# An attention and feed-forward kernel: new cuts at the end and in w_out, pair 0's loads on one queue, the first software load behind GpSimd's constants, five stores in halves

## Chip, cores and metric

One core of a Trainium2 chip. The metric is the device time of one execution in microseconds (us). A kernel is timed several times; medians are given with the lowest and highest run. The profile comes from one execution of each kernel, and its "span" runs from the first to the last instruction that the trace holds. The measured time is about 2 us longer than the span, that difference called **outside the span** below. The granted clock is the share of its full clock that the chip grants TensorE.

## The reference

Linear attention in 8 batches, 8 heads, 576 rows and 64 columns, an RMS norm, then a feed-forward part on 4608 tokens:

```python
kv  = einsum('bhsd,bhse->bhde', k, v)
out = einsum('bhsd,bhde->bhse', q, kv)
x   = out / sqrt(mean(out*out, -1) + 1e-6) * g_norm     # then (4608, 512)
h   = x @ w_in                                          # 512 -> 2048
out = (h / (1 + exp(-1.702*h))) @ w_out                 # 2048 -> 512
```

## The kernel before

Heads are treated in pairs: four pairs per batch, "pair 0" being the first. TensorE runs the feed-forward part tile by tile (9 tiles of 512 tokens), with the attention of later batches fitted in between. What the change touches:

```python
LAST = ((0, DM // 2), (DM // 2, DM))          # last projection: 256 + 256 columns
...
for n in "kqv":                               # pair 0 of batch 0, f32, two hardware queues
    dst, src = ...
    if n == "v":
        nc.sync.dma_start(out=dst[:, 0:1], in_=src[:, 0:1])
        nc.scalar.dma_start(out=dst[:, 1:2], in_=src[:, 1:2])
    else:
        (nc.sync if n == "k" else nc.scalar).dma_start(out=dst, in_=src)
g_row = const.tile([1, D], F32)
nc.scalar.dma_start(out=g_row, in_=g_norm.unsqueeze(0))
nc.vector.memset(ident, 0.0)
nc.vector.memset(kvb[1], 0.0)
early_load("q", 0, 1, 2)                      # first load of GpSimd's software queue
nc.gpsimd.affine_select(out=ident, ...)       # the mask
...
for c in range(1, NPAIR):                     # pairs 1 to 3, software queue, f32 -> f16
    for n in "qkv"[c == 1 :]:
        early_load(n, 0, c, c + 1)
load_w_in(...)                                # five requests, same queue
nc.vector.memset(ones2, 0.0)                  # and two blocks of ones
...
def project(mo, fo): ...                      # one matmul of 512 columns into os[mo]
def store_rest(mo, n0, n1):                   # one store on Sync, one on ScalarE
    ...
    queue = (nc.sync, nc.scalar)[g]
    queue.dma_start(out=rows, in_=osb[g * R : (g + 1) * R, mo, n0:n1])
def project_last(mo):
    for i, (n0, n1) in enumerate(LAST):       # 16 matmuls, copy, store
        ...
        copy = nc.vector.tensor_copy if i else nc.scalar.copy
        copy(osb[:, mo, n0:n1], o)
        store_rest(mo, n0, n1)
if deep:                                      # tile 0
    steps = [(mo, 4 * i + k) for i in range(4) for mo in range(4) for k in range(4)]
...
elif t < B:                                   # tiles 2 to 7: one store of 1 MB
    nc.sync.dma_start(out=out[t * S : t * S + SM, :].rearrange(...), in_=osb)
...
for c in (0, 2):
    load_half("k", 1, c, c + 2)
    load_half("v", 1, c, c + 2)
    load_w_out(8 + 2 * c, 12 + 2 * c)         # last quarter of w_out in one request
```

Of the kernel before, what the change touches and what calls it, by code (L numbers as in the profile page):

```python
# [8 lines left out]
F32 = mybir.dt.float32  # L9
# [3 lines left out]
P = 128  # L13
# [3 lines left out]
def kernel(  # L17
# [10 lines left out]
    nc = tc.nc  # L28

    B, H, S, D = q.shape  # L30
    DM = H * D
    DFF = moe_w_in.shape[1]
    NPAIR = H // 2
    FO = DFF // P
    KO = DM // P
    EPS = 1e-6
    SM = 512
    J = SM // P
    R = S - SM
    assert R == 64 and B * R == SM and KO == NPAIR and 2 * D == P  # L40
    NT = B + 1
    LAST = ((0, DM // 2), (DM // 2, DM))
    EARLY = 2
    PE_ = 96
    NJ = S // PE_
# [11 lines left out]
    opool = ctx.enter_context(tc.tile_pool(name="opool", bufs=2))  # L57
# [18 lines left out]
    ones2 = const.tile([P, P], F16)  # L76
# [10 lines left out]
    def early_src(n, b, c0, c1):  # L87
        return srcs[n][b, 2 * c0 : 2 * c1].rearrange("h (p j) d -> p h (j d)", j=NJ)

    def early_load(n, b, c0, c1):  # L90
        nc.gpsimd.dma_start(  # L91
            out=raw[n][0:PE_, c0:c1, :].rearrange("p c (l x) -> p (c l) x", l=2),
            in_=early_src(n, b, c0, c1),
        )
# [15 lines left out]
    def load_half(n, b, c0, c1):  # L110
        for l in range(2):
            nc.gpsimd.dma_start(  # L112
                out=raw[n][l * PH : (l + 1) * PH, c0:c1, 0 : NH * D],
                in_=srcs[n][b].rearrange("(c l) (p j) d -> l p c (j d)", l=2, j=NH)[l][:, c0:c1],
            )
# [5 lines left out]
    def load_q(b, queue=nc.sync):  # L121
        t = stage.tile([P, H, J * D], F32, name="qf", tag="qf")
        queue.dma_start(out=t, in_=q[b, :, 0:SM, :].rearrange("h (p j) d -> p h (j d)", j=J))
        r = stage.tile([P, 4, D], F32, name="qrf", tag="qrf")
        for g in range(2):
            queue.dma_start(
                out=r[g * R : (g + 1) * R],
                in_=q[b, 4 * g : 4 * g + 4, SM:S, :].rearrange("h p d -> p h d"),
            )
        staged[b] = (t, r)  # L130
# [12 lines left out]
    for n in "kqv":  # L143
        first[n] = stage.tile([P, H, J * D], F32, name=f"{n}f", tag=f"{n}f")
        first[n] = first[n].rearrange("p h x -> p (h x)")[0:PE_, 0 : 2 * NJ * D]
        dst, src = first[n].rearrange("p (h x) -> p h x", h=2), early_src(n, 0, 0, 1)
        if n == "v":
            nc.sync.dma_start(out=dst[:, 0:1], in_=src[:, 0:1])
            nc.scalar.dma_start(out=dst[:, 1:2], in_=src[:, 1:2])
        else:  # L150
            (nc.sync if n == "k" else nc.scalar).dma_start(out=dst, in_=src)
    g_row = const.tile([1, D], F32)
    nc.scalar.dma_start(out=g_row, in_=g_norm.unsqueeze(0))
    nc.vector.memset(ident, 0.0)
    nc.vector.memset(kvb[1], 0.0)
    early_load("q", 0, 1, 2)
    nc.gpsimd.affine_select(
        out=ident,
        in_=ident,
# [3 lines left out]
        pattern=[[-1, P]],  # L163
        channel_multiplier=1,
    )
    def load_w_in(f0, f1, k0=0, k1=KO):
        nc.gpsimd.dma_start(
            out=w_in_sb[:, k0:k1, f0 * P : f1 * P],
            in_=moe_w_in[k0 * P : k1 * P, f0 * P : f1 * P].rearrange(
                "(ko ki) f -> ki ko f", ki=P  # L170
            ),
        )

    for c in range(1, NPAIR):
        for n in "qkv"[c == 1 :]:
            early_load(n, 0, c, c + 1)
    load_w_in(0, 4, 0, 2)
    load_w_in(0, 4, 2, KO)
    load_w_in(4, GROUP)
# [1 line left out]
    load_w_in(10, FO)  # L181

    nc.scalar.preload_act_table_set("natural_log_exp_and_others")
    nc.vector.memset(ones2, 0.0)
    nc.vector.memset(ones2[0:D, 0:D], 1.0)
    nc.vector.memset(ones2[D:P, D:P], 1.0)
    nc.vector.memset(eps_t, EPS)
    one_t = const.tile([1, 1], F32)
    nc.vector.memset(one_t, 1.0)
# [2 lines left out]
    def load_w_out(f0, f1):  # L192
        nc.gpsimd.dma_start(
            out=w_out_sb[:, f0:f1, :],
            in_=moe_w_out[f0 * P : f1 * P, :].rearrange("(fo ki) n -> ki fo n", ki=P),
        )
# [252 lines left out]
    def dense(t, units1, units2, group, deep, hid=None):  # L449
        hid = hid or Hidden(t)  # L450
        gT = hid.gT
        if group and t:
            order = [(ko, fo) for part in (range(4), range(4, group)) for ko in (0, 1) for fo in part]
            order += [(ko, fo) for ko in range(2, KO) for fo in range(group)]
            for ko, fo in order:
                pool = (ps_h, "hT") if fo < 3 else (ps_a, "att") if fo == 3 else (ps_o, "o")
                hid.mm(ko, fo, *pool)
            for fo in range(group):
                hid.gate(fo)
        for fo in range(FO):  # L460
            if fo >= group:
                for ko in range(KO):
                    hid.mm(ko, fo)
                hid.gate(fo)
            for u in units1.get(fo, ()):
                u()

        osb = opool.tile([P, 4, DM], F32, name="osb", tag="osb")
        os = {}

        def project(mo, fo):
            if fo == 0:
                pool, tag = (ps_h, "hT") if deep and mo < 2 else (ps_o, "o")
                os[mo] = pool.tile([P, DM], F32, name="o", tag=tag)
            nc.tensor.matmul(  # L475
                os[mo],
                gT[:, fo, mo * P : (mo + 1) * P],
                w_out_sb[:, fo, :],
                start=(fo == 0),
                stop=(fo == FO - 1),  # L480
            )
            if fo == FO - 1:
                by_act = mo % 2 if deep or t == B else 0 < t < B - 1 and mo < 2
                copy = nc.scalar.copy if by_act else nc.vector.tensor_copy
                copy(osb[:, mo, :], os[mo])  # L485
                if t == B:
                    store_rest(mo, 0, DM)

        def store_rest(mo, n0, n1):
            for g in range(2):  # L490
                rows = out[(2 * mo + g) * S : (2 * mo + g + 1) * S, n0:n1]
                if 2 * mo + g < EARLY:
                    p0 = SM % PE_
                    rows = rows[bass.DynSlice(NJ * p0 + SM // PE_, R, step=NJ), :]
                else:
                    rows = rows[SM:S, :]
# [5 lines that stand above are left out]
            for i, (n0, n1) in enumerate(LAST):  # L502
                o = ps_a.tile([P, n1 - n0], F32, name="oh", tag="att")
                for fo in range(FO):
                    nc.tensor.matmul(  # L505
                        o,
                        gT[:, fo, mo * P : (mo + 1) * P],
                        w_out_sb[:, fo, n0:n1],
                        start=(fo == 0),
                        stop=(fo == FO - 1),  # L510
                    )
                copy = nc.vector.tensor_copy if i else nc.scalar.copy
                copy(osb[:, mo, n0:n1], o)
                store_rest(mo, n0, n1)

        if deep:
            steps = [(mo, 4 * i + k) for i in range(4) for mo in range(4) for k in range(4)]
        else:
            steps = [(mo, fo) for mo in range(4 - (t == B)) for fo in range(FO)]
        for n, (mo, fo) in enumerate(steps):  # L520
            project(mo, fo)
            for u in units2.get(n, ()):
                u()
        if t == B:
            project_last(3)
        if t < EARLY:

            n = 0
            while n < SM:
                mo, j, p = n // P, n // PE_, n % PE_  # L530
                m = min((mo + 1) * P, (j + 1) * PE_) - n
                nc.sync.dma_start(
                    out=out[t * S : (t + 1) * S, :][bass.DynSlice(NJ * p + j, m, step=NJ), :],
                    in_=osb[n % P : n % P + m, mo, :],
                )
                n += m
        elif t < B:
            nc.sync.dma_start(
                out=out[t * S : t * S + SM, :].rearrange("(p j) m -> p j m", j=J), in_=osb
            )  # L540


    a0 = First(0)
# [70 lines left out]
    for c in (0, 2):  # L614
        load_half("k", 1, c, c + 2)
        load_half("v", 1, c, c + 2)
        load_w_out(8 + 2 * c, 12 + 2 * c)
    load_q(2, nc.gpsimd)

    nc.gpsimd.dma_start(out=g_all, in_=g_norm.unsqueeze(0).to_broadcast([P, D]))  # L620

    live = {0: a0}

    def start(b):
# [2 lines left out]
    for t in range(NT):  # L627
# [32 lines left out]
        elif b < B:  # L660
# [21 lines left out]
            at2(36, of(b, "ss", NPAIR))  # L682
            at2(36, of(b, "apply", NPAIR))
        dense(t, u1, u2, (GROUP, 5)[t] if t < 2 else 0, t == 0, None if t else d0)


# [28 lines left out]
```

## Time and profile before

| | before |
|---|---|
| time, median of 3 runs | 287.84 us (287.82 to 288.01) |
| span of the profiled run | 285.6 us |
| that run's time outside the span | 2.14 us |
| TensorE's last matmul ends | 281.65 us |
| end of the span after that, the "tail" | 3.94 us |

The tail and the time outside are worked out from the trace's nanoseconds: 285.595 - 281.654, and 287.74 (the profiled run) - 285.595. The views round, so a tail here and below can differ by 0.01 from what they give.

In the lines of the profile PE is TensorE, PEld its weight loads, DVE VectorE, ACT ScalarE, POOL GpSimd and SP Sync; L91 is line 91 of the kernel, x4 a count. The DMA issues of the first 2.4 us (destination and source, queue, count, KB each, us from issue to landing). ACTq is ScalarE's queue, SPq is Sync's, POOLq is GpSimd's software queue:

```profile
kf<-in_k_dram SPq DMA_DIRECT2D x1, 288.0 KB, 4.4
qf<-in_q_dram ACTq DMA_DIRECT2D x1, 288.0 KB, 4.6
vf<-in_v_dram SPq DMA_DIRECT2D x1, 144.0 KB, 4.8
vf<-in_v_dram ACTq DMA_DIRECT2D x1, 144.0 KB, 5.1
qraw<-in_q_dram POOLq DMA_DIRECT2D x1, 144.0 KB, 5.5
```

All five requests are open together. The timelines (start, us, engine, line, operation, in brackets the idle time before it and what ended it) show when GpSimd makes the first software request, and how TensorE meets the last of w_out:

```profile
1.29 0.82 POOL L91 DMA_DIRECT2D qraw<-in_q_dram  x1 [0.84 <-POOLq L699]
...
42.13 1.29 PE L475 MATMUL o<-w_out_sb,gT 128*128 128x512 f16 x4
43.26 0.38 PE L259 MATMUL outT<-qT,kvb 128*128 128x512 f16 x1
```

### The profile page before, as it was taken

What the parts mean: (1) busy time and instruction counts of PE and PEld (TensorE: products, weight loads), DVE (VectorE), ACT (ScalarE), POOL (GpSimd) and SP (SyncE); (2) the same over time, 40 slices, a digit from 0 to 9 for tenths busy, and PEclk for the clock granted to TensorE, in tenths of its full rate; (3) what the DMA queues carried; (4) which work ended last, traced back from release to release, by engine and by line L of the source; (5) the groups of instructions that cost most, each with busy time, mean ns of one, the idle gap of its engine ahead of it and who ended that gap; (6) DMA issues with size and microseconds to landing.
All of it is one profiled execution on the core that took longest, in us unless ns stands there. A gap on an engine that the chain in (4) does not pass through costs nothing.

```text
span 285.6 us, 4343 instructions
## 1 busy us (share of the span) xinstructions
PE 278.9 (98%) x1717; PEld 135.4 (47%) x1717; DVE 119.3 (42%) x233; ACT 156.1 (55%) x273; POOL 56.0 (20%) x78
## 2 busy tenths in 40 slices
PE   7899999999999999999999999999999999999994
PEld 2444544455445544554455445544454444444443
DVE  2540656527651757156713862286327400110011
ACT  2697349766565646574558436762666375026400
POOL 8931541111211121112011401140002000000000
PEclk9999999999999999999999999999999999999999
DMA  8999999995589339963698269924501220021022
GB/s 175 204 205 205 206 251 238 234 268 103 123 166 254 58 73 197 252 116 73 191 197 176 37 186 171 228 54 147 119 2 37 73 112 0 0 92 57 0 73 73
DMA packets 53349, 38.76 MB, mean 136 GB/s; under 512 B 31138, under 2 KB 50850, under 8 KB 52562
## 3 DMA queue, kind: packets, MB, share of 16 engines
q0 software_dynamic: 14944, 15.58, 32.7%
q1 hardware_dynamic: 37664, 21.94, 31.0%
q10 hardware_dynamic: 722, 0.97, 1.2%
q8 instruction: 13, 0.21, 0.3%
q14 instruction: 6, 0.05, 0.0%
HBM read 36.73 MB, written 9.44 MB: 162 GB/s over the span
## 4 chain that ended last, share of the span: by engine, by line
PE 85%; DMA 11%; ACT 1%; POOL 1%; DVE 0%; issue 0%
PE o L475 39%; PE hT L438 39%; DMA w_out_sb<-in_moe_w_out_dram 10%; PE kvp L227 2%; PE outR L291 2%; DMA qf<-in_q_dram 2%; PE oh L505 1%; PE ss L339 1%; PE idle L554 0%; PE q L393 0%; POOL vbuf L112 0%; PE outT L259 0%; ACT qraw L545 0%; PE outT L270 0%; POOL qraw L91 0%
## 5 line engine op out<-in xcount | busy, mean ns | idle before, releaser
L475 PE MATMUL o<-w_out_sb,gT 128*128 128x512 f16 x560 | 130.9, 379 | 0.1
L447 ACT ACTIVATE gT<-hT 128x512 f16<-128x512 f32 x144 | 84.5, 599 | 76.5 <-PE hT L438 76.4
L438 PE MATMUL hT<-xT,w_in_sb 128*128 128x512 f16 x512 | 116.2, 379 | 0.0
L438 PEld LDWEIGHTS <-w_in_sb 128*128 128x128 f16 x576 | 54.5, 98 | 62.3 <-DMA w_in_sb<-in_moe_w_in_dram 0.5
L475 PEld LDWEIGHTS <-gT 128*128 128x128 f16 x560 | 52.8, 98 | 56.5 <-issue 0.7
L485 DVE COPY osb<-o 128x512 f32<-128x512 f32 x20 | 13.8, 691 | 62.3 <-PE o L475 62.3
L323 POOL TENSOR_TENSOR x<-xr,g_all 128x512 f16<-128x512 f32 x12 | 15.3, 1272 | 71.2 <-DVE xr L316 47.2
L218 DVE COPY kpad<-kraw 64x576 f16<-64x576 f16 x56 | 25.0, 446 | 2.0 <-DMA kraw<-in_k_dram 0.7
L302 DVE TENSOR_REDUCE sum<-sq 128x8 f32<-128x512 f16 x24 | 15.8, 679 | 19.9 <-ACT sq L299 19.9
L240 DVE CAST kvb<-kvp 64x128 f16<-64x128 f32 x28 | 8.1, 288 | 36.5 <-PE kvp L227 36.3
L316 DVE TENSOR_TENSOR xr<-outR,sum 128x512 f32<-128x512 f32 x24 | 15.5, 686 | 11.1 <-ACT sum L313 11.1
L112 POOL DMA_DIRECT2D kraw<-in_k_dram x16 | 9.9, 624 | 49.4 <-DVE kpad L218 43.5
L112 POOL DMA_DIRECT2D vbuf<-in_v_dram x16 | 9.7, 608 | 34.0 <-PE kvp L227 29.3
L323 DVE TENSOR_TENSOR x<-xr,g_all 128x512 f16<-128x512 f32 x12 | 15.2, 1268 | 0.7
L299 ACT ACTIVATE sq<-outR 128x512 f16<-128x512 f32 x24 | 13.6, 590 | 2.0 <-PE outR L291 1.6
L227 PEld LDWEIGHTS <-kpad 128*128 128x128 f16 x252 | 11.0, 98 | 7.0 <-DVE kpad L218 0.9
L438 PE MATMUL hT<-x_rem,w_in_sb 128*128 128x512 f16 x64 | 14.0, 379 | 0.0
L279 ACT ACTIVATE sq<-outT 128x512 f16<-128x512 f32 (+1 forms) x16 | 7.7, 481 | 10.5 <-PE outT L259 9.1
L485 ACT COPY osb<-o 128x512 f32<-128x512 f32 x15 | 8.7, 581 | 6.3 <-DMA out_dram<-osb 6.3
L227 PE MATMUL kvp<-vbuf,kpad 128*128 128x64 f16 x252 | 11.9, 193 | 0.1
L312 ACT ACTIVATE sum<-sum,eps_t 128x16 f32<-128x16 f32 x12 | 3.7, 308 | 15.0 <-DVE sum L302 15.0
L341 ACT ACTIVATE ln<-ss,eps_t 128x512 f32<-128x512 f32 (+1 forms) x16 | 9.4, 584 | 4.2 <-PE ss L339 4.1
(62 smaller groups left out, 140.8 us busy)
## 6 DMA issues: line engine op xcount, KB each, us to landing
out_dram<-osb SPq DMA_DIRECT2D x6, 1024.0 KB, 4.3
qf<-in_q_dram SPq DMA_DIRECT2D x5, 1024.0 KB, 8.4
kraw<-in_k_dram POOLq DMA_DIRECT2D x12, 288.0 KB, 5.9
vbuf<-in_v_dram POOLq DMA_DIRECT2D x12, 288.0 KB, 6.1
w_out_sb<-in_moe_w_out_dram POOLq DMA_DIRECT2D x4, 512.0 KB, 14.1
out_dram<-osb SPq DMA_DIRECT2D x6, 192.0 KB, 5.6
qf<-in_q_dram POOLq DMA_DIRECT2D x1, 1024.0 KB, 12.7
kraw<-in_k_dram POOLq DMA_DIRECT2D x7, 144.0 KB, 9.5
```

Source lines behind the costliest of these rows:

```text
L112: nc.gpsimd.dma_start(out=raw[n][l * PH : (l + 1) * PH, c0:c1, 0 : NH * D], in_=srcs[n][b].rearrange("(c l) (p j) d -> l p c (j d)", l=2, ...
L218: nc.vector.tensor_copy(out=kpad[r, c, :, l * D : (l + 1) * D], in_=kraw[r, c, 0 : NH * D].rearrange("p (j d) -> p j d", j=NH),)
L227: nc.tensor.matmul(self.kvp[:, c, :], kpad[:, c, j, :], vbuf[:, c, j * D : (j + 1) * D], start=(j == 0), stop=(j == NH - 1),)
L299: nc.scalar.activation(sq, t, AFT.Square)
L302: nc.vector.tensor_reduce(out=self.sum2[:, j % 2, :], in_=sq.rearrange("p (h d) -> p h d", h=H), op=ALU.add, axis=mybir.AxisListType.X,)
L316: nc.vector.tensor_mul(xr[:, i], self.o[j + i].rearrange("p (h d) -> p h d", h=H), s2[:, i, :].unsqueeze(2).to_broadcast([P, H, D]),)
L323: (nc.vector if i else nc.gpsimd).tensor_mul(self.x16[:, j + i, :].rearrange("p (h d) -> p h d", h=H), xr[:, i], g_all.unsqueeze(1).to_bro ...
L341: nc.scalar.activation(ln[:, 0:n], t[:, 0:n], AFT.Ln, bias=eps_t, scale=1.0 / D)
L438: nc.tensor.matmul(self.h[fo], w_in_sb[:, ko, fo * P : (fo + 1) * P], self.x[:, ko], start=(ko == 0), stop=(ko == KO - 1),)
L447: nc.scalar.activation(self.gT[:, fo, :], self.h[fo], AFT.Gelu_apprx_sigmoid)
L475: nc.tensor.matmul(os[mo], gT[:, fo, mo * P : (mo + 1) * P], w_out_sb[:, fo, :], start=(fo == 0), stop=(fo == FO - 1),)
L485: copy(osb[:, mo, :], os[mo])
```

## The change

Its intent: copy and store less after the last matmul; take the last wait for w_out away; let pair 0's loads run through one hardware queue in the order of use; and keep the software queue's first load out of their way until GpSimd has written its constants. In addition the stores of tiles 2 to 6 go out in halves. The diffs here and below are shortened: `...` and words in brackets stand for what is left out. `store(t, j0, j1)` is one request on Sync for the rows j0 to j1 of a tile.

```diff
-    LAST = ((0, DM // 2), (DM // 2, DM))
+    LAST = ((0, 3 * P), (3 * P, DM))
@@ pair 0
-        if n == "v":
-            nc.sync.dma_start(out=dst[:, 0:1], in_=src[:, 0:1])
-            nc.scalar.dma_start(out=dst[:, 1:2], in_=src[:, 1:2])
-        else:
-            (nc.sync if n == "k" else nc.scalar).dma_start(out=dst, in_=src)
+        nc.sync.dma_start(out=dst, in_=src)
@@ GpSimd
-    early_load("q", 0, 1, 2)
     nc.gpsimd.affine_select(...)
+    nc.gpsimd.memset(ones2, 0.0)
+    nc.gpsimd.memset(ones2[0:D, 0:D], 1.0)
+    nc.gpsimd.memset(ones2[D:P, D:P], 1.0)
-        for n in "qkv"[c == 1 :]:
+        for n in "qkv":
-    nc.vector.memset(ones2, 0.0)                  (and its two blocks)
@@ stores
+                elif t in HALVED and mo % 2:      # HALVED = (2, 3, 4, 5, 6)
+                    store(t, mo - 1, mo + 1)
-        elif t < B:
-            nc.sync.dma_start(out=out[...], in_=osb)
+        elif t < B and t not in HALVED:
+            store(t, 0, J)
@@ tile 0's projection
-            steps = [(mo, 4 * i + k) for i in range(4) for mo in range(4) for k in range(4)]
+            steps = [(mo, 4 * i + k) for i in range(3) for mo in range(4) for k in range(4)]
+            steps += [(mo, f + k) for f in (12, 14) for mo in range(2) for k in range(2)]
+            steps += [(mo, 12 + k) for mo in (2, 3) for k in range(4)]
@@ w_out
-        load_w_out(8 + 2 * c, 12 + 2 * c)
+        if c == 0:
+            load_w_out(8, 12)
+        else:
+            load_w_out(12, 14)
+            load_w_out(14, FO)
```

More of the change, by code (lines that the diff above doesn't have):

```diff
@@ L183 @@
     nc.scalar.preload_act_table_set("natural_log_exp_and_others")
-    nc.vector.memset(ones2, 0.0)
-    nc.vector.memset(ones2[0:D, 0:D], 1.0)
-    nc.vector.memset(ones2[D:P, D:P], 1.0)
     nc.vector.memset(eps_t, EPS)
@@ L466, in dense @@
                 u()
-        osb = opool.tile([P, 4, DM], F32, name="osb", tag="osb")
+        osb = osbs[t] = opool.tile([P, 4, DM], F32, name="osb", tag="osb")
         os = {}
@@ L536, in dense, with store @@
                 n += m
-        elif t < B:
-            nc.sync.dma_start(
-                out=out[t * S : t * S + SM, :].rearrange("(p j) m -> p j m", j=J), in_=osb
-            )
+        elif t < B and t not in HALVED:
+            store(t, 0, J)
+    def store(t, j0, j1):
+        nc.sync.dma_start(
+            out=out[t * S : t * S + SM, :].rearrange("(p j) m -> p j m", j=J)[:, j0:j1],
+            in_=osbs[t][:, j0:j1],
+        )
     a0 = First(0)
@@ L616 @@
         load_half("v", 1, c, c + 2)
-        load_w_out(8 + 2 * c, 12 + 2 * c)
+        if c == 0:
[3 more added lines that the diff above has]
+            load_w_out(14, FO)
     load_q(2, nc.gpsimd)
     nc.gpsimd.dma_start(out=g_all, in_=g_norm.unsqueeze(0).to_broadcast([P, D]))
+    osbs = {}
+    HALVED = (2, 3, 4, 5, 6)
     live = {0: a0}
```

## The prediction

> **What bounds the kernel now.** I read the page first (engine shares and the chain that ended last), then the tables by stretch, the timeline of TensorE and of GpSimd, and the waits of TensorE and its weight loads.
>
> ```profile
> span 285.6 us, 4343 instructions
> PE 278.9 (98%) x1717; PEld 135.4 (47%) x1717; DVE 119.3 (42%) x233; ACT 156.1 (55%) x273; POOL 56.0 (20%) x78
> PE 85%; DMA 11%; ACT 1%; POOL 1%; DVE 0%; issue 0%
> ```
>
> TensorE is busy 98% of the span, with two large groups of 576 and 560 matmuls of 512 columns at a pace of 0.216 us (64 of them take 13.81 us in the chain). The change adds and removes no such matmul. So all that can move is the rest: the start, the few stalls of TensorE on loads, and the tail after its last matmul. The run is 287.84 us for a span of 285.6, so I carry 2.2 us outside the span as a constant.
>
> The start, from the table by stretch (columns: PE, PEld, DVE, ACT, POOL busy, granted clock, DMA share, GB/s moved):
>
> ```profile
> 2.00:3.00 1.00, 1.00 (x4) 0.35 (x3) 0.00 (x0) 0.73 (x1) 0.91 (x3) 1.00 0.67 166
> 3.00:3.50 0.50, 0.50 (x3) 0.22 (x2) 0.00 (x0) 0.50 (x1) 0.50 (x2) 1.00 1.03 390
> 3.50:4.00 0.50, 0.50 (x3) 0.18 (x2) 0.00 (x0) 0.06 (x1) 0.50 (x2) 1.00 1.13 313
> 4.00:4.50 0.50, 0.50 (x3) 0.15 (x1) 0.00 (x0) 0.00 (x0) 0.50 (x2) 1.00 1.11 252
> 5.50:6.00 0.50, 0.42 (x2) 0.00 (x0) 0.17 (x1) 0.50 (x1) 0.50 (x2) 1.00 1.28 203
> 7.00:12.00 5.00, 4.81 (x86) 2.56 (x85) 2.72 (x8) 2.94 (x6) 4.86 (x8) 1.00 1.31 200
> ```
>
> From 3.0 us the DMA engines are full (share over 1). The 200 GB/s from 5.5 us on is not slower: those loads read f32 and write f16, and the count is of the bytes written, so some 400 GB/s are read. TensorE looks busy here, but 21 of its matmuls are dummies that keep it warm. What really holds it is the stream of loads:
>
> ```profile
> 12.82 0.38 PE L376 MATMUL kv<-vbuf,kraw 96*64 96x64 f16 x12 [0.67 <-DMA vbuf<-in_v_dram]
> 16.36 4.90 PEld L438 LDWEIGHTS <-w_in_sb 128*128 128x128 f16 x24 [0.28 <-DMA w_in_sb<-in_moe_w_in_dram]
> 23.34 4.94 PEld L438 LDWEIGHTS <-w_in_sb 128*128 128x128 f16 x24 [0.24 <-DMA w_in_sb<-in_moe_w_in_dram]
> ```
>
> Pair 3's v ends a wait of 0.67 us at 12.8, then w_in chunks end waits of 0.28 and 0.24. Whatever TensorE wins before 12.8 us beyond that 0.67 is lost again, unless the stream itself comes earlier. The last such meeting is the chain of waits around 42 us:
>
> ```profile
> 33.04 9.53 DMA w_out_sb<-in_moe_w_out_dram
> 42.57 0.04 issue
> 42.61 0.81 PE o L475 x3
> ```
>
> The last quarter of w_out is requested at 33.04 and lands at 42.57. The TensorE timeline has 4 matmuls from 42.13 where the next piece starts at 43.26: 1.13 us for 4 x 0.216 = 0.86, so a stall of 0.27. After that TensorE shows no wait at all until its end at 281.65. The tail:
>
> ```profile
> 281.65 0.02 issue
> 281.68 0.42 DVE osb L513
> ```
>
> then the store of the second half (issue at 282.1) and the end at 285.6.
>
> **What the Trainium skill says.** "DMA: Bandwidth & Descriptors", section "Issuing engines are not separate DMA queues": loads started on several engines run on the same 16 DMA engines and interleave; more queues save sequencer time only. The trace agrees: with two hardware queues and the software queue the engines are simply full from 3.0 us. So putting k, q and v on one queue changes their order, not the sum of the work. Same page, "Queues, rings and completion order": each engine takes the queues in turn by packet; that the fourth load then shares with pair 0 fits the first software load's 5.5 us to landing, against 5.0 for the next. "TensorE: Matmul & The Clock Gate", section "Back-to-back issue gap", gives some 81 ns a matmul at 128 columns in a real stream; this trace has 9 products of 64 columns with new weights in 0.26 us (29 ns each) and 12 transposes of 96 columns in 0.40 (33 ns), so the measurement decides and I take 55 ns at 128 columns. "VectorE: DVE Perf Modes", section "Zero memsets can be issued as uint32", explains the row of 128x64 uint32 in 0.112 us for a 128x128 f16 zero; on GpSimd the same memset is f16 and no run here shows its length yet.
>
> **The change, part by part.**
>
> 1. End: the last projection is cut 384 + 128 columns, not 256 + 256. TensorE: 16 x (0.163 + 0.055) = 3.49 us against 32 matmuls in 3.51 in the chain: nothing. The last VectorE copy shrinks from 256 to 128 columns. A 512-column copy takes 0.69 and a 256-column one 0.42, so 0.27 for 256 columns, and 0.42 - 0.13 = 0.29: **-0.13 us**. The last two stores carry 32 KB, not 64; stores of 64 KB land in 2.1 us and of 128 KB in 2.4 to 2.7, so perhaps **-0.05**, since at this size most is fixed. The larger first part: TensorE ends it 16 x 0.055 = 0.88 us before the last matmul, the ScalarE copy of 384 columns is between 0.37 and 0.58 (0.48), and each store issue takes some 0.5, so the queues are free 0.1 after TensorE's end, before the last copy ends at 0.31. No new wait.
>
> 2. w_out in two requests of 256 KB, and the projection of tile 0 ordered so that its last quarter is first used as chunks 12 and 13 for two row blocks, then 14 and 15. At 200 GB/s written, 256 KB take 1.3 us: chunks 12 and 13 land near 41.3, TensorE asks at 42.30. Chunks 14 and 15 still land at 42.57, but are asked for four matmuls and one outT later: 42.30 + 5 x 0.216 = 43.4. The stall goes: **-0.27 us**. One more request costs GpSimd 0.76, beside a queue whose requests wait 9.5 us for their data: nothing. The row block 0 copy is two matmuls (0.43 us) later, 1.5 us before its bank is needed.
>
> 3. Stores of tiles 2 to 6 in two halves. In the table of waits the store queue waits for VectorE's copies, and nobody on the path waits for a store. The first half goes behind the transposes of x on the same in-order queue, so cannot delay them; the second half leaves 0.5 MB less ahead of the next transposes of q. **0**.
>
> 4. Pair 0: k, q, v on the Sync queue. Requests at 0.74, 1.20 and 1.66 (the first two issues here stand 0.46 apart), where q went at 0.74 from ScalarE. q still has k ahead of it: k + q are 576 KB whether they share or follow each other, so q lands near 5.3 as now, v earlier than 6.3 by up to 0.5 since the software load no longer shares. The first products wait for q and ScalarE's cast, so start at 6.2 as now.
>
> 5. The software queue: the first load is requested at 1.29 now. Before it will stand the mask (0.31) and three memsets; constants of one column on GpSimd take 0.10, VectorE's 128-column ones 0.11, so I take 0.1 to 0.2 each. That is an issue near 1.9; the mask already stood before the second request, so requests 2 to 9 and w_in come 0.3 later. Data: the engines have 864 KB of pair 0 to move until past 5 us, and a request needs under 5.0 us from issue to landing, of which 0.74 is its own data; so the engines should not run dry. The stream keeps its end: **0**, with an uncertainty of half a microsecond either way (below).
>
> Sum: -0.13 - 0.05 - 0.27 = -0.45, so 287.84 - 0.45 = 287.4 us.
>
> **The rivals.**
> (a) The stream ends earlier. From 3.5 to 5.5 us the rate dips from 390 to about 250 GB/s while q, v and the first software load mix. If order cures the dip, (390 - 270) x 2 us = 240 KB, some 0.6 us, come back; TensorE has a 0.67 wait at 12.8 to take it from. For: the dip is there. Against: the page's section says mixing alone costs nothing, and part of the dip is software data counted half. Then 286.8.
> (b) The stream ends later. With q requested 0.46 later the ramp from 1.7 to 3.0 us may be thinner, and the first software data may come after pair 0 has drained. For: the first software request now needs 5.5 us. Against: 864 KB are enough to fill the gap. Delay 0.3 to 0.6 us, handed on by the waits at 12.8, 16.4 and 23.3: 287.8 to 288.0.
> (c) A new wait in the steady part: a half store colliding with a transpose of x, whose result TensorE needs about 0.5 us after it lands. Even 0.3 us in five tiles is 1.5 us, so 288.9. Against: queue order. I give it 5%.
>
> **Range and chances.** Most weight on the sum, a quarter each on (a) and (b): 287.4, from 286.7 to 288.2. Two per cent is 5.8 us, and everything outside TensorE's steady work that this change touches is under 2 us; so within 2% has 0.97, faster 0.015, slower 0.015.
>
> **What would show it.** Step 1 right: the last copy near 0.29 us, TensorE's last matmul to the end of the span 0.15 to 0.2 shorter than now (3.95). Step 2 right: no piece of tile 0's projection is held by w_out, four matmuls take 0.86. Steps 4 and 5 right: q's cast starts within 0.2 of 5.33, pair 3's v ends its wait near 12.8, the w_in waits stay. Wrong: pair 3's product starting before 12.4 (rival a) or after 13.1 (rival b); or any wait of TensorE after 50 us (rival c).

## More of the kernel before

At the very end, the table of Sync's own waits (us in total, times, longest) has a wait in the kernel's last line, L710, for the last stores:

```profile
SPq L710 <- DMA out_dram<-osb: 1.6, 1, 1.6
```

## The result, and the profile after

After: 286.82 us median of 4 runs (286.67 to 287.19); before in the same rounds: 287.83 (287.82 to 288.01). The ratio is 0.9965, interval 0.9948 to 0.9982. A ratio is the mean time of one kernel's fast runs over that of the other's of the same rounds, so not quite the ratio of the medians. The time fell by 1.0 us where 0.45 was forecast; a later repeat (e12) gave -1.16. It is in the range and within 2%, but half of the gain had no step in the prediction, and so it is in part luck that the time lies in the range.

The page of the kernel after, its span and the engine shares of the chain that ended last:

```profile
span 284.9 us, 4354 instructions
...
PE 93%; POOL 2%; DMA 2%; DVE 1%; issue 0%
```

The chain's share on DMA falls from 11% to 2%: the w_out load no longer ends a wait of TensorE. Where the 1.04 us between the two profiled runs (287.74 and 286.70) lie:

| | before | after | difference |
|---|---|---|---|
| TensorE's last matmul ends | 281.65 | 281.50 | -0.15 |
| tail to the end of the span | 3.94 | 3.42 | -0.52 |
| outside the span | 2.14 | 1.77 | -0.37 |

So TensorE's work, where the prediction put -0.27, gives the smallest part. The tail, where it put -0.18, gives half. And more than a third lies where no engine's record is.

**The start.** The issues of the first 2.4 us of the kernel after, columns as before:

```profile
kf<-in_k_dram SPq DMA_DIRECT2D x1, 288.0 KB, 3.4
qf<-in_q_dram SPq DMA_DIRECT2D x1, 288.0 KB, 4.0
vf<-in_v_dram SPq DMA_DIRECT2D x1, 288.0 KB, 4.8
qraw<-in_q_dram POOLq DMA_DIRECT2D x1, 144.0 KB, 5.1
```

k lands a full microsecond earlier; q, requested at 1.21, lands at 5.2 (before 5.3); v, requested at 1.69, lands at 6.5 (before 6.3), so later, not earlier. The table by stretch of the kernel after (columns as in the prediction, last one GB/s) shows that the dip in the rate is still there, although only one hardware queue carries pair 0:

```profile
3.50:4.00 0.50, 0.50 (x3) 0.18 (x2) 0.00 (x0) 0.00 (x0) 0.50 (x2) 1.00 1.23 243
4.00:4.50 0.50, 0.50 (x3) 0.15 (x1) 0.33 (x1) 0.00 (x0) 0.50 (x2) 1.00 0.93 218
4.50:5.00 0.50, 0.50 (x2) 0.15 (x1) 0.37 (x1) 0.00 (x0) 0.50 (x1) 1.00 1.02 258
```

The same stretches before had 313, 252 and (not in the prediction's lines) 267 GB/s. Its timelines of GpSimd, of TensorE with its weight loads, and of the last copy:

```profile
1.79 0.82 POOL L91 DMA_DIRECT2D qraw<-in_q_dram  x1
...
12.90 0.38 PE L372 MATMUL kv<-vbuf,kraw 96*64 96x64 f16 x12 [0.70 <-DMA vbuf<-in_v_dram]
...
16.51 4.86 PEld L434 LDWEIGHTS <-w_in_sb 128*128 128x128 f16 x24 [0.35 <-DMA w_in_sb<-in_moe_w_in_dram]
...
23.41 4.98 PEld L434 LDWEIGHTS <-w_in_sb 128*128 128x128 f16 x24 [0.20 <-DMA w_in_sb<-in_moe_w_in_dram]
...
42.24 1.03 PE L471 MATMUL o<-w_out_sb,gT 128*128 128x512 f16 x4
43.10 0.38 PE L255 MATMUL outT<-qT,kvb 128*128 128x512 f16 x1
...
281.53 0.29 DVE L511 COPY osb<-oh 128x128 f32<-128x128 f32 x1 [2.80 <-PE oh L503]
```

The software request moves from 1.29 to 1.79, pair 3's product from 12.82 to 12.90, and the waits for w_in stay. The four matmuls at w_out now take 43.10 - 42.24 = 0.86: no stall. The last copy takes 0.29. At the end, Sync's wait in the last line (now L720) is split in two:

```profile
SPq L720 <- DMA out_dram<-osb: 1.2, 2, 0.9
```

That change of shape was the first hint to the order of waits at the program's end, below.

### The profile page after: what moved, and what is told of

Same layout as the page of the kernel before. It is cut to its first block, busy times and chain, and to the rows that moved or that the text cites. A ratio compares the mean times of both kernels' runs of the same rounds, so it can differ in the third digit from the quotient of the medians.

```text
span 284.9 us, 4354 instructions
## 1 busy us (share of the span) xinstructions
PE 279.1 (98%) x1717; PEld 135.1 (47%) x1717; DVE 118.9 (42%) x230; ACT 156.1 (55%) x273; POOL 57.1 (20%) x82
## 4 chain that ended last, share of the span: by engine, by line
PE 93%; POOL 2%; DMA 2%; DVE 1%; issue 0%
PE hT L434 44%; PE o L471 42%; PE kvp L223 3%; DMA vbuf<-in_v_dram 2%; PE outR L287 2%; PE oh L503 1%; POOL kraw L91 1%; PE ss L335 1%; POOL qraw L91 1%; DVE kpad L214 1%; PE outT L255 0%; POOL vbuf L91 0%; PE q L412 0%; PE outT L266 0%; PE idle L558 0%
## 6 DMA issues: line engine op xcount, KB each, us to landing
kraw<-in_k_dram POOLq DMA_DIRECT2D x12, 288.0 KB, 6.9
vbuf<-in_v_dram POOLq DMA_DIRECT2D x12, 288.0 KB, 5.5
```

## The experiments

Twelve runs. Kernels are compared only within the same rounds. Medians, us:

| run | median (lowest to highest) | before | ratio, 95% interval |
|---|---|---|---|
| e1_end | 287.75 (287.65 to 287.87) | 287.97 | 0.9992, 0.998 to 1.0005 |
| e2_wout | 287.74 (287.47 to 287.93) | 287.97 | 0.9993, 0.9979 to 1.0007 |
| e3_start | 287.57 (287.51 to 287.68) | 287.97 | 0.9987, 0.9975 to 1.0 |
| e4_halves | 287.69 (287.61 to 288.0) | 287.97 | 0.9992, 0.998 to 1.0005 |
| e5_oneq | 289.3 (287.96 to 292.04) | 287.9 | 1.0067, 1.0023 to 1.0112 |
| e6_behind | 288.26 (287.93 to 288.44) | 287.9 | 1.0012, 1.0 to 1.0024 |
| e7_nostart | 287.54 (287.12 to 287.57) | 287.9 | 0.9987, 0.9974 to 1.0 |
| e8_two_more (wrong result) | 287.29 (287.01 to 288.08) | 287.9 | 0.9982, 0.9971 to 0.9993 |
| e9_halved7_grow | 287.15 (287.05 to 287.35) | 287.9 | 0.9973, 0.9959 to 0.9986 |
| e10_rot2_stores | 287.53 (287.19 to 287.79) | 287.9 | 0.9983, 0.997 to 0.9995 |
| e11_again (wrong result) | 287.35, one run | 287.9 | none |
| e12_after_again | 286.74 (286.61 to 287.07) | 287.9 | 0.9959, 0.9947 to 0.9972 |

The profiled run of each, cut as above. "Numbers" are explained under e8; "outside" is that of the profiled run, and all timed runs of a kernel agree with it within 0.1 us.

| run | TensorE ends | tail | numbers | outside |
|---|---|---|---|---|
| before | 281.65 | 3.94 | 2, 3 | 2.14 |
| after | 281.50 | 3.42 | 6, 7 | 1.77 |
| e1_end | 281.93 | 3.71 | 2, 3 | 2.11 |
| e2_wout | 281.38 | 3.94 | 2, 3 | 2.14 |
| e3_start | 281.80 | 3.97 | 1, 2 | 1.80 |
| e4_halves | 281.79 | 3.78 | 7, 0 | 2.12 |
| e5_oneq | 286.16 | 3.96 | 1, 2 | 1.80 |
| e6_behind | 281.99 | 3.94 | 2, 3 | 2.11 |
| e7_nostart | 281.35 | 3.61 | 7, 0 | 2.16 |
| e8_two_more | 282.54 | 3.76 | 0, 1 | 1.77 |
| e9_halved7_grow | 281.93 | 3.61 | 7, 0 | 1.77 |
| e10_rot2_stores | 281.61 | 3.79 | 0, 1 | 1.78 |
| e11_again | 281.74 | 3.81 | 0, 1 | 1.79 |
| e12_after_again | 281.52 | 3.44 | 6, 7 | 1.77 |

Tails with the same cut and the same numbers agree within 0.05 us, and the time outside within 0.1. TensorE's end does not repeat like that: the span of the kernel before lies between 285.3 and 286.3 us in the 29 runs, that of the kernel after between 284.8 and 285.4 in its nine. So a few tenths in the column "TensorE ends", from one profile each, show nothing by themselves; e1, with no edit before the last projection, ends 0.28 later than before.

### One part at a time: e1 to e4

The theory was that the four parts add up, and that what the prediction missed sits in one of them; the rival was that it comes only from them together. Each run has one part on the kernel before.

e1_end, the last projection cut in 384 + 128 columns:

```diff
-    LAST = ((0, DM // 2), (DM // 2, DM))
+    LAST = ((0, 3 * P), (3 * P, DM))
```

> Only the end part: the last projection cut 384 + 128 columns. My sum: the last VectorE copy 0.29 us instead of 0.42, landing of the last store 0.05 to 0.1 earlier, so 0.2 us less in all, with TensorE's last matmul at 281.65 as before. Rival (the tail is worth more than its copy): the changed kernel's tail after the last matmul is 3.43 us against 3.95; if all of that comes from the cut, this run is 0.5 us faster with the tail near 3.4. If the tail gain has another source (the queues used at the start, the half stores), the tail here stays near 3.75.

The tail is 0.23 shorter (3.94 to 3.71). The chain's last copy shows 0.13 of it:

```profile
281.95 0.29 DVE osb L513
```

It was 0.42. The other 0.10 comes behind the copy: from TensorE's end to the last data there are 2.04 us instead of 2.33, so the stores of 32 KB instead of 64 give another 0.16, and from the last data to the end of the span 0.07 is lost again (1.67 for 1.61). In the time, -0.22.

e2_wout, only the w_out requests and tile 0's order:

```diff
-            steps = [... for i in range(4) ...]
+            steps = [... for i in range(3) ...]
+            steps += [(mo, f + k) for f in (12, 14) for mo in range(2) for k in range(2)]
+            steps += [(mo, 12 + k) for mo in (2, 3) for k in range(4)]
-        load_w_out(8 + 2 * c, 12 + 2 * c)
+        load_w_out(8, 12)                      (c == 0), else 12 to 14 and 14 to 16
```

> Only the w_out part: the last 512 KB in two requests and the order of steps that uses chunks 12 and 13 first. My sum: the 0.27 us stall near 42.3 us goes, TensorE's last matmul ends at 281.38 and the run is 0.27 us faster. Rival (the stall is only moved to chunks 14 and 15, or to the next load): a wait of the same size shows between 42 and 47 us and the run is as before within 0.1.

TensorE ends at 281.38 instead of 281.65, the stall is gone, the tail and the time outside are as before: -0.27 in the profile, -0.23 in the time.

e3_start, both halves of the start:

```diff
-            (nc.sync if n == "k" else nc.scalar).dma_start(out=dst, in_=src)   (and v in halves)
+        nc.sync.dma_start(out=dst, in_=src)
-    early_load("q", 0, 1, 2)                  (moved behind the mask and GpSimd's three memsets)
```

> Only the start: k, q, v of pair 0 in one hardware queue, the software queue's first load behind GpSimd's constants. By the profile of the changed kernel the load stream is 0.1 us later (pair 3's product at 12.90 instead of 12.82), so this run's span is 0.1 us longer. Rival: the time outside the span, 2.14 us in the profiled run of before and 1.77 in the changed kernel, belongs to the start; then this run is 0.25 us faster although its span is 0.1 longer.

The time is 0.40 lower, and none of it is in TensorE's work. Its timeline has pair 3's product even later than the prediction's limit of 13.1:

```profile
13.21 0.38 PE L372 MATMUL kv<-vbuf,kraw 96*64 96x64 f16 x12 [0.69 <-DMA vbuf<-in_v_dram]
```

and TensorE ends at 281.80. What falls is the time outside the span, from 2.14 to 1.80. That was carried as a constant.

e4_halves, only the stores of tiles 2 to 6 in halves:

```diff
+                elif t in HALVED and mo % 2:
+                    store(t, mo - 1, mo + 1)
-        elif t < B:
+        elif t < B and t not in HALVED:
```

> Only the stores of tiles 2 to 6 in halves. My sum: 0, since no store is on the path; within 0.1 us of before, TensorE's last matmul at 281.65, tail 3.95. Rival: fewer or differently spread transfers shorten what comes after the last instruction, and the run is 0.2 to 0.4 us faster with the same last matmul.

-0.28 in the time, where 0 was predicted; the interval reaches 1.0005. No wait of TensorE changes in the steady part. But the tail, some 180 us after the first of these stores (at 104.8), is 0.16 shorter (3.78), with the old cut of the last projection. Why, e8 to e11 show.

The four differences of medians add up to -0.22 - 0.23 - 0.40 - 0.28 = -1.13, the whole change has -1.0 to -1.16. The sums agree, but each part alone is at the edge of what the timing resolves, and three parts at once (e7, below) gave less than their sum. So the times alone do not show that the parts add up; it takes the profile to tell what each does.

### The two halves of the start: e5 and e6

e5_oneq has pair 0 on one queue and leaves the software queue's load first:

```diff
-        if n == "v": ... else: ...             (two hardware queues)
+        nc.sync.dma_start(out=dst, in_=src)
```

> Only the one-queue half of the start: k, q, v of pair 0 all requested by Sync; the software queue's first load where it was. The whole start part measured 0.4 us faster with a span only 0.1 shorter: the time outside the span fell from 2.11 (2.07 to 2.14 in nine runs of before) to 1.79. Theory 1: that fall comes from the engine that issues the loads (ScalarE now requests one small row instead of three loads); then this run has 1.8 outside the span. Theory 2: it comes from GpSimd's order (mask and constants ahead of its first request); then this run stays at 2.1 and gains nothing.

It is slower, and erratic: three of six runs at 287.96 to 288.32 with a granted clock of 0.998 to 1.0, three at 290.28 to 292.04 with 0.98 to 0.994. The profile fell in one of the latter. From its DMA issues, its TensorE timeline and its table by stretch:

```profile
vf<-in_v_dram SPq DMA_DIRECT2D x1, 288.0 KB, 6.8
```

```profile
9.13 0.53 PE L372 MATMUL kv<-vbuf,kraw 96*64 96x64 f16 x12 [2.16 <-DVE vbuf L543]
```

```profile
5.00:10.00 5.00, 2.84 (x35) 1.57 (x34) 1.22 (x3) 0.83 (x1) 3.20 (x5) 0.88 1.19 192
10.00:15.00 5.00, 5.00 (x55) 2.37 (x55) 1.27 (x4) 2.29 (x4) 3.72 (x6) 0.50 1.28 200
15.00:20.00 5.00, 5.00 (x36) 2.07 (x36) 2.66 (x6) 3.50 (x6) 2.43 (x4) 0.59 1.28 204
```

v takes 6.8 us to land instead of 4.8. The first product of k and v waits 2.16 us, TensorE is busy for only 2.84 of 5 us, and the granted clock (behind the five busy times) goes 0.88, 0.50, 0.59. TensorE then looks busy all the time and does half the work. The Trainium skill says in "DMA: Bandwidth & Descriptors", section "Queues, rings and completion order", that each engine goes round its queues by packet. By that the software load would get one turn in two beside one hardware queue, and one in three beside two. The packets in the traces fit this in part only. Both first software loads were requested at 1.3 us. In e5 the software queue's first data packet starts at 3.82, and from 4.0 to 4.5 us it moves 40 packets beside 48 of pair 0; in the kernel before its first packet starts at 4.89. But one turn in three does not explain none at all until then, and e5's first software load itself lands later too, at 8.3 us instead of 6.8. That v shares with the software load in e5 is shown; why it does so only with one hardware queue stays open. The three faster runs of e5 have no profile, so whether v is late there too is not known.

e6_behind is the other half alone: two hardware queues, the software load behind the constants:

```diff
-    early_load("q", 0, 1, 2)
     nc.gpsimd.affine_select(...)
+    nc.gpsimd.memset(ones2, 0.0)              (and two blocks of ones)
```

> Only the other half of the start: ones2 set by GpSimd and the software queue's first load requested behind the mask and these memsets; k, q, v on the two hardware queues as before. Theory 1 (issuing engines): 2.1 outside the span, time within 0.1 of before. Theory 2 (GpSimd's order): 1.8 outside the span, 0.3 faster. For the stream of loads: pair 3's product should start within 0.1 of 12.8[...].

+0.36 us, with an interval that reaches 1.0. In its profile the weight loads wait more for w_in; first the line of the kernel before, then that of e6 (us in total, times, longest):

```profile
PEld L438 <- DMA w_in_sb<-in_moe_w_in_dram: 0.5, 2, 0.3
```

```profile
PEld L438 <- DMA w_in_sb<-in_moe_w_in_dram: 1.7, 4, 0.5
```

But e1 and e4, which have the start of the kernel before, wait 1.5 and 1.6 us in four pieces as well, and the kernel after 0.5 in one profile and 1.2 in the other (e12). So these waits vary by themselves, and it is not shown that the later requests cost anything.

In the medians one half of the start costs 1.4 us and the other 0.36, and both together gain 0.40. Of these only e5's slow runs stand clear of the noise: three of its six, 2.4 to 4.1 us over the kernel before; the other three lie 0.1 to 0.4 over it. The one queue needs the later software load, as e5 against e3 shows. In e3's profile TensorE ends 0.14 later than before, which is within what kernels with an unchanged start show (e4 0.14, e1 0.28), and the 0.34 outside the span more than pays for it. The prediction treated the two halves as independent zeros.

e6 also says which half owns the time outside the span: 2.11 with two hardware queues, while e5 has 1.80 with one.

### All but the start: e7

```diff
(the edits of e1, e2 and e4 together on the kernel before)
```

> All but the start: end, w_out and half stores together. Parts alone: end -0.22, w_out -0.23, halves -0.28 in the medians, so -0.7 if they add up and 287.25; by the traces, the tail after the last matmul should be 3.94 - 0.23 (end) - 0.16 (halves) = 3.55, TensorE without a stall on w_out, and 2.1 outside the span. If the half stores act only through noise, the tail is 3.7 and the run about 287.5.

The time is 0.36 lower; TensorE's end is 281.35, tail 3.61, outside 2.16. The tail is near the expected 3.55, but the median gives only half of the -0.7 expected from the three parts. The profiled run has 0.6 less than that of before; the gap to the median is not explained. What the start adds to this is -0.42 between the profiled runs (287.12 and 286.70): -0.39 outside the span, -0.19 in the tail with the same cut of the projection, and +0.16 in TensorE's end. Between the medians it is more, -0.8 (-1.16 for e12 less -0.36); e7's profiled run was the fastest of its runs.

### The end of the program: e8 to e11

After its last store, Sync waits for the hardware queues' eight completion semaphores, 0 to 7 in this order, each in an instruction of its own, before the final barrier. The packed trace holds these instructions, though no view prints them. Every hardware-queue DMA takes the next of the eight in turn. So which two the last pair of stores holds depends on how many such DMAs the whole kernel has: the "numbers" above, ScalarE's store first and Sync's second. The kernel before has 76 such DMAs, so its last one holds number 3 (counted from 0); the kernel after has 80, five stores more and one load of v less, so number 7.

The theory: waits that stand behind the last landing store are walked through one by one although long satisfied. With 6, 7 almost none are left, with 0, 1 six more. The rival: the shorter tail comes from something else in the kernel after (half stores that leave the queues emptier). e8 turns the numbers by two and leaves the rest:

```diff
+    spare = const.tile([1, 2 * D], F32)
+    def turn_sems():
+        for i in range(2):
+            nc.sync.dma_start(out=spare[:, i * D : (i + 1) * D], in_=g_norm.unsqueeze(0))
             if t + 2 < B:
                 at1(f0, load_q, t + 2)
+            if t == 4:
+                at1(f0, turn_sems)
                 at1((10 if t == 1 else 9) + 4, load_kv, t + 2)
```

> The changed kernel with two added loads of 256 bytes on the Sync queue in tile 4, to a tile nobody reads. Theory (the tail's extra gain is the place of the last store's semaphore): the program ends with the Sync engine waiting for eight hardware-queue semaphores in the order 0 to 7; the last landing store holds number 2 in before (five waits left after it), 7 with the halves alone (none left), 6 in the changed kernel (one left). Two more loads turn the numbers on by two, so the last store holds 0 and seven waits stand behind it: six more than now, at some 0.045 us each the tail grows from 3.42 to 3.7 and the run is 0.25 us slower than the changed kernel's 286.8, near 287.1. Rival (the tail's gain belongs to the stores themselves): tail 3.42 as in the changed kernel.

The tail went from 3.42 to 3.76. But the result was wrong (relative error 0.8728), and the reason is in the diff: the inserted condition swallowed the line below it, so the loads of k and v ran only for tile 4. The DMA issues show it, first the kernel after, then e8:

```profile
kraw<-in_k_dram POOLq DMA_DIRECT2D x12, 288.0 KB, 6.9
```

```profile
kraw<-in_k_dram POOLq DMA_DIRECT2D x4, 288.0 KB, 8.4
```

Eight of twelve loads of k are missing, and as many of v. So e8's total time means nothing; its tail, far behind the last of these loads, may be read, and was to be confirmed by a kernel with a right result. e11 ran the same file again:

```diff
(none against e8)
```

> The run that gave a wrong result, repeated unchanged for one look. If the wrong result belongs to the kernel (the two 256-byte loads beside the rest), it is wrong again; if it belonged to that one execution, whose first software load landed 6.3 us after its request, it is right now. Tail again 3.7 to 3.8.

The same error to the last digit, which fits a missing load and not a race; tail 3.81.

e9_halved7_grow turns the numbers by one, by halving tile 7's store as well, and moves g_row's load to Sync, so that ScalarE requests nothing at the start:

```diff
-    nc.scalar.dma_start(out=g_row, in_=g_norm.unsqueeze(0))
+    nc.sync.dma_start(out=g_row, in_=g_norm.unsqueeze(0))
-    HALVED = (2, 3, 4, 5, 6)
+    HALVED = (2, 3, 4, 5, 6, 7)
```

> The changed kernel, with tile 7's store in halves too and the 256-byte row of g_norm requested by Sync, so that ScalarE requests nothing at the start. Two readings. Outside the span: with three loads requested by ScalarE it was 2.12, with one 1.78. If each start request of ScalarE costs some 0.17, this run has 1.6; if it is the number of packets in ScalarE's queue (402 now, 722 before), it stays at 1.77; if it is only the long q load, 1.77 as well. Tail: the last landing store now holds semaphore 7, with no wait behind it, so 3.42 less one wait of 0.045, about 3.4. Time 286.5 to 286.8, the best of all if the first reading holds.

Here I was wrong in the size: I expected a tail near 3.4 with ScalarE's store at number 7, and it was 3.61, as e7's with the same numbers; the time of 286.5 to 286.8 was missed too. Sync's store holds 0 then; Sync is held there until it lands, and has still to walk through 1 to 7, from 284.25 to 284.62 us, though ScalarE's store had landed at 284.34. The time outside the span stays 1.77, so it is not the number of ScalarE's requests at the start as such.

e10_rot2_stores turns the numbers by two, with a right result:

```diff
-        queue.dma_start(out=t, in_=q[b, :, 0:SM, :]...)
+        for h0, h1 in ((0, 4), (4, 8)) if b == 6 else ((0, 8),):
+            queue.dma_start(out=t[:, h0:h1], in_=q[b, h0:h1, 0:SM, :]...)
-                queue = (nc.sync, nc.scalar)[g]
+                queue = (nc.sync, nc.scalar)[g] if mo == 3 else nc.sync
-    HALVED = (2, 3, 4, 5, 6)
+    HALVED = (2, 3, 4, 5, 6, 7)
```

> The changed kernel, with one more store half and one q load in two pieces, which turns the semaphores by two as in the wrong run but with ordinary transfers only, and with the stores of the last tile's first three row blocks all requested by Sync, which takes some 190 of the 402 packets out of ScalarE's queue. Tail: the last landing store holds semaphore 0, seven waits behind it, so 3.42 + 6 x 0.045 = 3.7, as the wrong run's 3.76; the rival says 3.42. Outside the span: 1.77 if the start requests set it, 1.55 if the packets of ScalarE's queue do. Time near 287.1.

The tail is 3.79, near e8's and e11's, and Sync's wait in the last line has one piece again:

```profile
SPq L724 <- DMA out_dram<-osb: 1.6, 1, 1.6
```

That is the shape and length of the kernel before, not the two pieces of the kernel after. From 6, 7 to 0, 1 the tail grows by about 0.36 us for six more satisfied waits, so 0.06 us each (an estimate from these two tails, and the step that the traces show; the 0.045 in the expectations was too small). It then gives 3.43 + 4 x 0.06 = 3.67 for 2, 3 with the new cut, where e1 has 3.71. More half stores did not shorten it, so the rival falls.

The recorded waits show the walk itself. In the kernel before Sync passes number 2 at 284.38 us, as ScalarE's store lands, and then 3 to 7 at 284.44, 284.50, 284.56, 284.62 and 284.68, though its own store had landed at 284.07. In the kernel after it passes 6 at 283.95 and 7 at 284.01. From number 7 to the end of the span both need 0.92. So four steps fewer, 0.24 us, stand in the traces directly.

e10's time outside the span is 1.78 with 162 packets in ScalarE's queue instead of 402, so it is not the number of these packets either. Its time is 0.8 over e12's; 0.36 of that is this tail, 0.09 TensorE's end in the profiled runs; the rest is not explained.

### The kernel after again: e12

```diff
(none against the kernel after)
```

> The changed kernel unchanged, beside the others on one chip. 0.9 to 1.0 us faster than before, 1.77 outside the span, tail 3.42, no stall of TensorE on w_out; a second trace to tell how much pair 3's product and the w_in waits vary by themselves (12.8 to 13.1 expected).

-1.16 in the medians; tail 3.44, outside 1.77, TensorE's end 281.52: all three terms repeat. No experiment beat it.

## Why the prediction was right, and where its steps were not

The total stood in its range, by the sum of two steps that held and two terms that were missing. Its lower end was there for rival (a), which the runs refute, so that 286.82 fell inside is in part luck.

- **What bounds the kernel:** held. TensorE's work stays, and only start, stalls and tail moved.
- **Time outside the span as a constant:** failed. It is 2.06 to 2.20 us in all timed runs of the kernels where ScalarE requests a part of pair 0 (before, e1, e2, e4, e6, e7) and 1.72 to 1.83 in all where Sync requests all of it (after, e3, e5, e8 to e12). This is -0.34 us. Whether q or half of v does it, and by what means, stays open; e9 rules out that every start request of ScalarE's counts, e10 that the number of its packets does.
- **Step 1, the end:** the copy, -0.13, held. Stores and landing, -0.05, were nearer -0.10 (e1). The missing term is the order of the last waits: -0.29 more from e1's 3.71 to 3.42 with the same cut, 0.24 of it in four steps of 0.06. The forecast for the tail was 0.15 to 0.2 less, it was 0.52 less.
- **The 55 ns at 128 columns** in step 1: held. The second part's 16 matmuls take 281.50 - 280.62 = 0.88 us, 55 ns each (280.62 is worked out: ScalarE's copy of the first part starts at 280.63); the skill's 81 ns would have given 1.3.
- **Step 2, w_out:** held. Chunks 12 and 13 land at 41.34 (41.3 was worked out), the stall is gone, e2 alone -0.23 to -0.27. The stall is not the same in each build, though: 0.24 in e1, 0.12 in e4, 0.10 in e6, 0.02 in e3. It depends on when TensorE comes to this load and when the load lands, so -0.27 is its upper end.
- **Step 3, half stores, 0:** right for the steady part, no wait appeared. Wrong in the sum: five more DMAs turn the numbers of the last semaphores, -0.16 in e4's tail. It is an accident of counting, not a merit of halving.
- **Step 4, one queue, 0:** q's landing held (5.2), v's "earlier by up to 0.5" failed, it was 0.2 later. The premise, that the software load took its share from pair 0, had little behind it: in the trace of before the software queue's first data packet starts at 4.89 us, and pair 0's last one ends at 5.72. Alone, this step costs 1.4 us in the median of six widely spread runs (e5).
- **Step 5, later software requests, 0:** the request came at 1.79 as forecast (1.9), and pair 3's product at 12.90, near 12.8. Alone it measured +0.36 (e6), at the edge of the noise. Step 4 is harmless only with step 5, which the prediction did not say.
- **Rival (a)**, the dip cured by order: refuted. The dip is there with one queue, and the stream does not end earlier. Nor was the software load in the mix from 3.5 to 4.9 us, as the prediction read it. The time of 286.8 that it forecast came about by other causes.
- **Rival (b)**, a later stream: not in the kernel after, but e3 (13.21) and e9 (13.36) show it; builds that differ little place the stream's end within about half a microsecond.
- **Rival (c)**, a wait in the steady part: not seen.

## What to carry to other kernels

Subtract the span from the measured time for each kernel, not once, and look at the end of the compiled program: the order in which the last completion semaphores are awaited can move the time as much as the copy one is trying to shorten. One edit to the start can be safe only beside another, so test them apart and together before calling either free. And where a change moves several small things, cut the profiled runs into "last matmul", "tail" and "outside"; that told parts apart whose time intervals all touched 1. Tail and outside repeat, the end of TensorE's work varies from run to run.

## What the Trainium skill lacked or had wrong

- "TensorE: Matmul & The Clock Gate", section "Back-to-back issue gap": 81 ns a matmul at 128 columns in a real stream; here 16 matmuls with new weights each take 0.88 us, 55 ns each. The section's formula for isolated matmuls, about 56 ns, is nearer.
- "DMA: Bandwidth & Descriptors", section "Issuing engines are not separate DMA queues", says that issuing on several engines only saves sequencer time. Here, in one profile each and with the software load first in both, v landed 6.8 us after its request on one hardware queue (e5) and after 4.8 and 5.1 us in halves on two (before). So the choice of queues can change when a load lands; the cause stays open.
- No page was found that tells of the walk through satisfied completion waits at the end of a program: here about 0.06 us each, up to 0.36 us.
- "Runtime: NRT & Kernel Launch", section "The ~15µs preamble/postamble breakdown", lists what runs around a kernel and calls a gap of about 6.2 us between the profile's total and the reported time the same for every kernel. Neither it nor another page that was found tells that the choice of queue for the first loads moves the time outside the span: 2.06 to 2.20 against 1.72 to 1.83 us here.
- No page was found with GpSimd's time for a small memset: 128x128 f16 took 0.20 us and 64x64 0.14 to 0.15 (kernel after), against 0.11 on VectorE for each (kernel before; the larger as uint32).
